# First transform half: 24 narrow low parts moved from VectorE to GpSimd, with fixed PSUM banks and a new order

## The chip, the cores and the metric

The kernel runs on one core of a Trainium2 chip. The metric is device time in microseconds (us) of one launch; the kernel before was timed in three runs, and their median is the number that the change is compared with. A core has five engines that each work through a queue of their own, in order: TensorE (PE), VectorE (DVE), ScalarE (ACT), GpSimd (POOL) and SyncE (SP, which issues DMAs). They wait for each other only where data or a buffer demands it.

## The reference

```python
xn = layernorm(x)                                  # x: 2048 x 576
a  = xn @ dft_hid_re.T;   b = xn @ dft_hid_im.T    # 2048 x 576 each
y  = dft_seq_re @ a - dft_seq_im @ b               # the two 2048 x 2048 products
m  = relu(xn @ w1) @ w2                            # 576 -> 4608 -> 576
out = x + y + m
```

## The kernel before

Every float32 matrix is split into two float16 parts, a high part (the value cast to float16) and a low part (value minus high part), and a product is three float16 matmuls: high by high, high by low, low by high. Products are laid out as a seven-product block scheme (Strassen-Winograd): seven half-size products, with sums of blocks made beforehand or added afterwards.

The program runs through nine blocks of the MLP (`b` 0 to 8, four token groups `g` each; `t = 4b + g` up to 35), then through the transform. The transform has two halves. In the first half, for each token tile `t` from 0 to 15 and each half `z` of the columns, seven products (`pd`, L1392) of the normalised input and the hidden DFT matrix accumulate in three PSUM banks; they are collected (scaled by a half) into a float32 buffer `tb`, which has room for four tiles: tiles 4 to 7 use the places of 0 to 3. In the second half, sixteen units multiply blocks of the sequence DFT matrix (`cs`, its split parts) by these results (`R`, their split parts), L1478. Units 0 to 7 need tiles 0 to 7 only, so the first half is done in two goes: tiles 0 to 7 ahead of unit 0, tiles 8 to 15 around unit 7 and 8.

How one tile `t` of the first half becomes the right operand `R[t]`:

- `q:t:z:n` is product `n` (7 matmuls). A pair of tiles `t` and `t+2` is made by the products of `t`, so only `t` = 0, 1, 4, 5 stand in the table, 56 products in all.
- `c:t:z:n` collects it. Products 2, 3 and 7 are added by DVE from PSUM (L1405); the others are copied by ACT (L1407) or, marked V, by DVE (L1409).
- `sh:t:s` is a high part, on ACT (L1361). For `s` = 11, 21, 22 it is narrow, 128x288; for `s` = 0 it is wide, 128x1152: the four sums of blocks.
- `sl:t:s` is the low part, on DVE (L1365), with two inputs: the value in `tb` and the high part.
- `rs:t` makes the four sums in place in `tb` (DVE, L1371 to L1374), and so must come after the three narrow low parts of its tile have read it, and after the collection of product 4. The wide parts follow it.
- Unit steps: `oh` (ACT, L1015) and `ol` (DVE, L1019) split a left operand, `os` (DVE, L1447) makes its sums, `u:n:i:h` is one half (12 matmuls) of product `i` of unit `n`, `ue` evicts it, `ua` adds it to DRAM by a DMA issued on POOL.

The last MLP blocks and the first half, up to the end of unit 6, are written out word by word in a table, BLOCK8, which sets the order of all five queues; the rest is in another table, TURN. In BLOCK8 the words `p`, `f`, `h`, `l`, `x`, `H`, `L` are first-layer products and their activations, `m` a second-layer product (L809), `e` its eviction, `a:t:n` the DMA on POOL that adds it to DRAM, and `dl`, `dx`, `dL`, `dh`, `dw`, `ds` load, measure and split the hidden DFT matrix.

PSUM has eight banks. In the transform, `bank()` hands out tiles of two pools of four (`ps1`, `psd`) in turn, in the order in which the program asks.

Of the kernel before, what the change touches and what calls it, by code (L numbers as in the profile page):

```python
# [148 lines left out]
e:31:1 p:32:1:3 h:32:1:12 a:31:1 dl:2 l:32:1:12 m:31:3 f:32:1:3 dx:1:1 r:32:1 x:32:1 p:32:0:4
dx:1:0 p:33:0:5 h:32:0:12 m:31:2 l:32:0:12 f:33:0:5:A y:32:0 y:32:1 H:32:0 p:33:0:1 e:31:2:V  # L150
S:32:1 p:33:1:1 f:33:0:1:V L:32:0 e:31:3:A m:31:4 F:33:0 H:32:1 f:33:1:1:V m:31:5 e:31:4 L:32:1
a:31:4 dl:3 m:31:6 e:31:5 dx:2:1 a:31:5 m:32:0 e:31:6:V S:33:0 dx:2:0 a:31:6 p:33:1:6 F:33:1
m:32:1 f:33:1:6:V p:33:0:3 p:33:0:2 p:33:0:6 f:33:0:2 e:32:0:A p:33:1:2 f:33:0:6:V dL:0:0
h:33:0:11 f:33:0:3 m:32:2 f:33:1:2 r:33:0 e:32:1 h:33:1:11 l:33:1:11 a:32:1 p:33:0:7 l:33:0:11
dx:3:1 p:33:1:7 f:33:0:7 m:32:3 x:33:0 h:33:0:22 e:32:2:A l:33:0:22 dx:3:0 p:33:0:4 p:33:1:5
y:33:0 h:33:0:12 dR:0 l:33:0:12 H:33:0 m:32:4 f:33:1:5:V dp:0 S:33:1 f:33:1:7 L:33:0 p:34:0:1
e:32:3:A dL:0:1 p:33:1:4 f:34:0:1:A e:32:4 dh:0:0:1 p:33:1:3 h:33:1:12 dw:0:0:1 a:32:4 h:33:1:22
m:32:5 l:33:1:12 dh:0:0:0 f:33:1:3 F:34:0 r:33:1 dw:0:0:0 p:34:0:5 e:32:5 m:32:6 l:33:1:22
a:32:5 ds:0:0 dh:0:1:1 m:33:0 dh:0:1:0 dw:0:1:1 dh:0:0:2 x:33:1 p:34:0:6 e:32:6:A p:34:0:2
dh:0:0:3 f:34:0:5:V a:32:6 dw:0:0:2 m:33:1 dw:0:0:3 S:34:0 f:34:0:2 dL:0:2 p:34:0:3 f:34:0:6:V  # L160
dw:0:1:0 e:33:0:A p:34:0:7 y:33:1 h:34:0:11 e:33:1 H:33:1 p:34:1:2 f:34:0:7 a:33:1 p:34:1:1
l:34:0:11 h:34:0:22 L:33:1 p:34:0:4 F:34:1 f:34:1:1:A p:34:1:6 f:34:1:2 h:34:0:12 f:34:0:3
h:34:1:11 ds:0:1 m:33:2 r:34:0 m:33:3 e:33:2:A f:34:1:6:V dL:1:2 x:34:0 dh:0:1:3 m:33:4 dh:0:2:1
l:34:0:12 e:33:3:A y:34:0 dw:0:1:3 dh:0:1:2 m:33:5 e:33:4 H:34:0 l:34:0:22 a:33:4 dh:0:2:0
L:34:0 p:34:1:7 S:34:1 p:34:1:5 dw:0:2:0 p:35:0:1 F:35:0 f:34:1:5:V l:34:1:11 p:34:1:3
f:35:0:1:V dw:0:2:1 m:33:6 f:34:1:3 e:33:5 r:34:1 f:34:1:7 a:33:5 p:35:0:5 e:33:6:A x:34:1
p:34:1:4 h:34:1:22 a:33:6 l:34:1:22 p:35:0:2 y:34:1 h:34:1:12 f:35:0:5:A l:34:1:12 p:35:0:6
H:34:1 f:35:0:2 ds:0:2 p:35:1:1 h:35:0:11 S:35:0 p:35:1:2 m:34:0 F:35:1 l:35:0:11 dh:0:2:2
f:35:0:6:V dw:0:1:2 dh:0:2:3 p:35:0:7 dw:0:2:2 dL:1:0 e:34:0:V p:35:0:3 f:35:0:7 m:34:1 dw:0:2:3
h:35:0:22 f:35:0:3 L:34:1 r:35:0 p:35:0:4 p:35:1:5 e:34:1 h:35:0:12 S:35:1 m:34:2 x:35:0 a:34:1  # L170
y:35:0 dL:1:1 m:34:3 l:35:0:22 e:34:2:A f:35:1:1:V f:35:1:2 H:35:0 l:35:0:12 pm:0 m:34:4
e:34:3:A L:35:0 h:35:1:11 f:35:1:5:A p:35:1:6 e:34:4 p:35:1:3 l:35:1:11 f:35:1:6:A a:34:4
p:35:1:7 f:35:1:3 r:35:1 m:34:5 f:35:1:7 x:35:1 h:35:1:22 p:35:1:4 e:34:5 m:34:6 l:35:1:22
dh:1:2:0 a:34:5 y:35:1 h:35:1:12 dw:1:2:0 dh:1:1:1 m:35:0 dh:1:0:1 e:34:6:V dh:1:1:0 l:35:1:12
a:34:6 dh:1:0:0 m:35:1 dh:1:2:1 dw:1:1:1 dw:1:1:0 H:35:1 dw:1:2:1 dw:1:0:1 q:0:0:1 e:35:0:A
L:35:1 q:0:0:2 e:35:1 m:35:2 ds:1:1 a:35:1 q:0:0:5 e:35:2:A m:35:3 dw:1:0:0 dh:1:1:3 dh:1:1:2
ds:1:0 m:35:4 e:35:3:A dw:1:1:2 m:35:5 dh:1:0:2 e:35:4 dh:1:0:3 dw:1:0:2 m:35:6 a:35:4 e:35:5
dw:1:0:3 a:35:5 e:35:6:A dw:1:1:3 a:35:6 fs:0 q:0:1:1 ds:1:2 fm:0 c:0:0:5:A cl:0:0 q:1:0:1
c:0:1:1:A q:0:0:3 c:1:0:1:A c:0:0:1:V dh:1:2:2 q:1:0:6 c:0:0:2 dh:1:2:3 dw:1:2:2 q:0:0:6 sh:0:11
dw:1:2:3 c:1:0:6:A q:0:1:6 c:0:0:6:A sl:0:11 c:0:0:3 pa:0 q:0:0:7 c:0:1:6:A pb:0 sh:2:11 q:0:1:5  # L180
sl:2:11 c:0:0:7 pc:0 q:0:1:7 c:0:1:5:V pd:0 q:0:1:3 c:0:1:7 q:1:1:1 sh:2:22 c:0:1:3 sl:2:22
sh:2:21 q:1:1:2 c:1:1:1:A sl:2:21 rs:2 q:0:1:4 q:0:1:2 c:0:1:4:A sh:0:22 q:1:1:5 sh:2:0 sl:0:22
c:1:1:2 q:0:0:4 c:0:1:2 sh:1:21 sl:2:0 sh:0:21 q:1:1:6 c:1:1:5:A c:0:0:4:A q:1:1:3 sl:1:21
c:1:1:6:A sl:0:21 q:1:0:5 c:1:1:3 rs:0 sh:3:21 q:1:1:7 c:1:0:5:A q:1:0:3 sl:3:21 q:1:0:2 sh:0:0
c:1:1:7 c:1:0:3 q:1:1:4 c:1:0:2 sh:3:22 sl:0:0 sh:3:11 q:1:0:7 sh:1:11 c:1:1:4:A q:4:0:1 sh:1:22
c:1:0:7 sl:3:11 q:1:0:4 sl:1:22 c:4:0:1:A sl:3:22 q:4:0:2 rs:3 c:1:0:4:A fx:0 cl:0:2 oh:0 cl:0:3
q:4:0:5 cl:0:1 q:4:1:1 c:4:0:5:A ol:0 sh:3:0 q:4:1:5 sl:1:11 c:4:1:1:A q:4:1:2 sl:3:0 c:4:1:5:A
q:4:1:3 c:4:1:2 q:4:0:3 rs:1 sh:4:21 oh:1 q:4:1:6 q:5:0:1 sl:4:21 sh:1:0 ol:1 q:5:0:2 c:4:1:6:A
q:4:0:6 c:4:1:3 sl:1:0 sh:6:21 q:4:1:7 c:4:0:6:A q:4:0:7 c:5:0:1:A c:4:1:7 os:0:0 sh:6:22
q:5:0:6 q:4:1:4 c:4:0:7 c:5:0:6:A sl:6:22 os:0:1 q:4:0:4 c:4:1:4:A sh:4:22 q:5:0:7 c:4:0:2  # L190
# [24 lines left out]
ue:5:1 u:5:2:1 ol:40 ua:5:1 u:5:3:0 ue:5:2:V oh:41 cl:7:2 ol:41 u:5:3:1 u:5:4:0 oh:42 ue:5:3:A
ol:42 u:5:4:1 cl:7:1 os:6:1 u:5:5:0 oh:43 ue:5:4 ol:43 ua:5:4 u:5:5:1 os:6:2 u:5:6:0 oh:44
# [62 lines left out]
def kernel(  # L279
# [1188 lines left out]
    def block_product(n, i, ks):  # L1468
# [3 lines left out]
        if first and ks.start == 0:  # L1472
            places[n, i] = bank(f"p{n}_{i}")
# [131 lines left out]
```

## Time and profile before

| What | before |
|---|---|
| time, median of 3 runs | 1228.23 us (1227.09 to 1229.61) |
| span of the profiled execution (first to last instruction) | 1226.3 us |
| busy: PE, DVE, ACT, POOL | 1215.1, 1055.6, 726.2, 210.5 us |
| granted TensorE clock | 1.000 |

The profile gives the span of the execution that it shows; the time of a run includes what lies around the span, so the three runs lie 0.8 to 3.3 us above the span, the median 1.9 us. PE is busy in 99% of the span: the kernel can only lose or win in stretches where PE waits.

### The profile page before, as it was taken

Reading aid. Unit: us, or ns where it says so; the run is one execution under the profiler, and the core shown is the slowest. Engines: PE = TensorE matmul, PEld = TensorE weight load, DVE = VectorE, ACT = ScalarE, POOL = GpSimd, SP = SyncE. Lnnn points to the kernel's source line nnn. Section 1 sums busy time; section 2 is a strip of 40 time slices with the busy share of each in tenths; the row PEclk is TensorE's granted clock in tenths of the full one; section 3 lists DMA queues with packets and bytes.
Section 4 is the critical chain, followed back from the end, with each engine's and each line's share of the span. In section 5 each row is a group of like instructions: output and inputs, shape, how many; then the busy total and the mean of one; then the engine's idle time right before and its main releaser. Section 6 shows DMA issues by size and latency. Waiting matters only on the chain.

```text
span 1226.3 us, 26245 instructions
## 1 busy us (share of the span) xinstructions
PE 1215.1 (99%) x10516; PEld 999.2 (81%) x10516; DVE 1055.6 (86%) x2044; ACT 726.2 (59%) x1259; POOL 210.5 (17%) x274
## 2 busy tenths in 40 slices
PE   8999999999999999999999999998999999999998
PEld 8867888888888888888888888876777777777777
DVE  8877998888888889888988889999877769987885
ACT  7866765766757667657666547666444445534342
POOL 3432122122122222221121111200211110000000
PEclk9999999999999999999999999999999999999999
DMA  8997578688778777777666678631755532245441
GB/s 239 223 165 194 161 142 177 147 162 146 159 145 176 151 138 167 138 146 151 150 120 140 153 177 164 116 90 49 192 131 135 132 79 47 91 157 181 142 132 35
DMA packets 127051, 175.98 MB, mean 144 GB/s; under 512 B 48336, under 2 KB 88784, under 8 KB 126928
## 3 DMA queue, kind: packets, MB, share of 16 engines
q1 hardware_dynamic: 97696, 121.99, 34.0%
q0 software_dynamic: 28672, 51.92, 30.0%
q8 instruction: 82, 1.34, 0.5%
q10 hardware_dynamic: 560, 0.39, 0.1%
q14 instruction: 41, 0.34, 0.1%
HBM read 112.53 MB, written 56.62 MB: 138 GB/s over the span
## 4 chain that ended last, share of the span: by engine, by line
PE 94%; DVE 3%; DMA 1%; ACT 0%; issue 0%; SPq 0%; POOL 0%; DVEq 0%; ACTq 0%
PE bank L712 27%; PE p L809 27%; PE p L1478 26%; PE pd L1392 7%; PE p L588 4%; PE p L849 2%; DMA raw_w<-in_w_dram 1%; DVE R L1365 1%; PE p L1074 1%; DMA xT<-dbuf 0%; DVE w2s L1019 0%; DVE cs L1019 0%; DVE tb L1405 0%; DVE accs L1447 0%; DVE tb L1372 0%
## 5 line engine op out<-in xcount | busy, mean ns | idle before, releaser
L809 PE MATMUL p<-w2s,h 128*128 128x288 f16 x2688 | 357.0, 286 | 0.0
L1478 PE MATMUL p<-R,cs 128*128 128x288 f16 x2688 | 331.0, 286 | 2.5 <-DVE cs L1019 2.5
L1478 PEld LDWEIGHTS <-cs 128*128 128x128 f16 x2688 | 262.8, 98 | 69.6 <-DVE cs L1019 3.4
L809 PEld LDWEIGHTS <-h 128*128 128x128 f16 x2688 | 263.0, 98 | 62.0
L712 PEld LDWEIGHTS <-dbuf 128*128 128x128 f16 x1568 | 153.2, 98 | 20.7 <-issue 0.4
L712 PEld LDWEIGHTS <-wbuf 128*128 128x128 f16 x1568 | 153.4, 98 | 20.4
L1015 ACT ACTIVATE cs<-tb,sc_c 128x1024 f16<-128x1024 f32 x56 | 64.3, 1148 | 82.1 <-PE p L1478 59.8
L712 PE MATMUL bank<-xT,wbuf 128*128 128x256 f16 x896 | 110.4, 273 | 0.0
L712 PE MATMUL bank<-xT,dbuf 128*128 128x256 f16 x896 | 110.2, 273 | 0.0
L1019 DVE SCALAR_TENSOR_TENSOR cs<-tb,sc_c,cs 128x1024 f16<-128x1024 f32 x56 | 71.7, 1283 | 22.2 <-ACT cs L1015 21.3
L834 POOL DMA_DIRECT2D spill<-dbuf x70 | 61.3, 915 | 163.0 <-DVE dbuf L827 119.9
L712 PE MATMUL bank<-accs,dbuf 128*128 128x256 f16 x672 | 86.3, 273 | 0.2 <-DVE s L738 0.2
L712 PE MATMUL bank<-accs,wbuf 128*128 128x256 f16 x672 | 85.9, 273 | 0.0
L1015 ACT ACTIVATE cs<-accs,sc_c 128x1024 f16<-128x1024 f32 x40 | 45.9, 1148 | 58.5 <-PE p L1478 45.7
L759 DVE TENSOR_TENSOR h<-s,h 128x1024 f16<-128x1024 f32 x64 | 77.4, 1218 | 2.1 <-ACT h L753 2.1
L753 ACT ACTIVATE h<-s 128x1024 f16<-128x1024 f32 x64 | 66.6, 1050 | 13.1 <-DVE s L750 13.1
L1239 ACT ACTIVATE f<-f 128x1024 f32<-128x1024 f32 x64 | 67.2, 1050 | 4.0 <-DMA f<-in_cim_dram 3.0
L721 ACT ACTIVATE h<-accs 128x256 f16<-128x256 f32 x128 | 51.1, 410 | 29.9 <-DVE accs L736 23.7
L834 POOL DMA_DIRECT2D spill<-wbuf x42 | 39.5, 940 | 155.9 <-DVE wbuf L827 128.2
L1019 DVE SCALAR_TENSOR_TENSOR cs<-accs,sc_c,cs 128x1024 f16<-128x1024 f32 x40 | 51.2, 1282 | 13.7 <-ACT cs L1015 13.5
L823 ACT ACTIVATE dbuf<-p,c_ub 128x576 f32<-128x576 f32 x61 | 45.0, 738 | 25.5 <-PE p L809 25.5
L702 ACT ACTIVATE accs<-bank 128x256 f32<-128x256 f32 x97 | 36.9, 380 | 38.2 <-PE bank L712 15.6
(227 smaller groups left out, 1897.8 us busy)
## 6 DMA issues: line engine op xcount, KB each, us to landing
spill<-dbuf POOLq DMA_DIRECT2D x80, 288.0 KB, 4.5
f<-in_cre_dram SPq DMA_DIRECT2D x32, 512.0 KB, 5.0
f<-in_cim_dram SPq DMA_DIRECT2D x32, 512.0 KB, 5.0
spill<-wbuf POOLq DMA_DIRECT2D x48, 288.0 KB, 5.5
raw_w<-in_w_dram SPq DMA_DIRECT2D x18, 576.0 KB, 4.8
raw_w<-in_w_dram SPq DMA_DIRECT2D x17, 512.0 KB, 4.7
accs<-in_cim_dram SPq DMA_DIRECT2D x16, 512.0 KB, 4.6
tb<-in_cre_dram SPq DMA_DIRECT2D x16, 512.0 KB, 4.6
```

The costliest lines, as they stand in the source:

```text
L588: nc.tensor.matmul(ps[:, cols], w1s[b, i // 2][:, i % 2 * 2 + h, y], xT[g][:, h * KC + z, cols], start=(n == 0), stop=(n == len(wk) - 1),)
L712: nc.tensor.matmul(ps, l, r, start=first and m == 0, stop=m == len(todo) - 1, skip_group_check=not first,)
L721: nc.scalar.activation(next(high_low(q)), SOURCE[q], AF.Relu)
L753: order["s"] = nc.scalar.activation(next(high_low(SUMS)), stage_of(slice(1, 5)), AF.Copy).ins
L759: order["lo"] = nc.vector.tensor_tensor(lo, stage_of(slice(1, 5)), hi, ALU.subtract).ins
L809: nc.tensor.matmul(ps[:, c], h[:, x, qa, c * P : (c + 1) * P], w[:, y, qb], start=first and i == 0 and j == 0, stop=i == NQ - 1 and j == 2 ...
L834: nc.gpsimd.dma_start(spill[g, row, col], sums[g, row, col], accum_op=ALU.add)
L1015: nc.scalar.activation(hi, src, AF.Copy, scale=s)
L1019: nc.vector.scalar_tensor_tensor(lo, src, s, hi, ALU.mult, ALU.subtract)
L1239: nc.scalar.activation(f, f, AF.Abs, scale=2.0**-10, accum_out=sums_c[:, n, q : q + 1])
L1392: nc.tensor.matmul(ps, x[:, k, c * P : (c + 1) * P], dsp[z][:, a, y], start=first and m == 0, stop=m == len(PASSES) - 1, skip_group_check= ...
L1478: nc.tensor.matmul(ps, w[:, a, RANK[k]], r[:, c, RIGHT[rq]], start=first and k == 0 and j == 0, stop=k == HK - 1 and j == 2, skip_group_ch ...
```

## The change

- The 24 narrow low parts of tiles 0 to 7 get the word `:G` and run on GpSimd. They were 24 of 32 low parts on DVE there; the eight wide ones stay on DVE. Those of tiles 8 to 15 (in TURN) stay on DVE too.
- `bank()` is gone. All eight banks are allocated under numbers, and two tables say which three banks each chain of the first half and each unit uses.
- BLOCK8 is replaced up to unit 2 by the same words in a new order: 929 words in both, the only other difference being the `:G`. Among the moves: the first tile pair starts with product 2; the adds `a:35:4` to `a:35:6` go later, between the low parts on POOL; `a:31:4` goes from right behind its eviction to late in the last block; the loads `cl` of the left operands and the half units `u` are interleaved anew. From unit 3 on, and in TURN, the order is unchanged.

```diff
 BLOCK8 = """
...
-dw:1:2:3 c:1:0:6:A q:0:1:6 c:0:0:6:A sl:0:11 c:0:0:3 pa:0 q:0:0:7 c:0:1:6:A pb:0 sh:2:11 q:0:1:5
...
+sh:2:22 c:0:0:6:A q:0:0:7 q:0:1:4 c:0:1:4:A c:0:0:2 sh:0:11 sl:0:11:G c:0:0:3 q:1:1:1 sh:2:11
...
 """
+BANKS_D = "312 067 451 210 765 403 125 467 312 074 672 103 564 732 017 644"
+BANKS_C = "032 167 453 201 675 430 127 564 312 054 761 230 546 713 024 657"
...
-    def low_part(t, s):
+    def low_part(t, s, eng=nc.vector):
         hi, lo, src = part(t, s)
-        tt(lo, src, hi, ALU.subtract)
+        eng.tensor_tensor(lo, src, hi, ALU.subtract)
...
         if (t, z) not in chains:
-            chains[t, z] = [bank(f"pd{t}_{z}_{k}") for k in range(3)]
+            k = 2 * (t // TG * 2 + t % 2) + z
+            chains[t, z] = [bank_at[int(k)] for k in BANKS_D.split()[k]]
...
-            places[n, i] = bank(f"p{n}_{i}")
+            places[n, i] = bank_at[int(BANKS_C.split()[n][(0, 1, None, 2)[i]])]
...
-        pool["psd"] = tc.alloc_tile_pool(name="psd", bufs=4, space=PSUM)
+        pool["psd"] = tc.alloc_tile_pool(name="psd", bufs=1, space=PSUM)
+        for k in range(4, 8):
+            bank_at[k] = pool["psd"].tile([P, 512], F32, name=f"bank{k}")
```

Two places show what the table does to the queues. The first is DVE's queue where the first sums of a tile are made. In before these are the sums of tile 2 (`tb` has no numbers of its tiles), with a narrow low part (L1365, 128x288) after nearly every addition from PSUM (L1405):

```order
L1405 SCALAR_TENSOR_TENSOR tb_10831<-pd0_1_2_10814,tb_10831 128x288
L1365 TENSOR_TENSOR R2_10834<-tb_10831,R2_10834 128x288 x2
L1371 TENSOR_TENSOR tb_10831<-tb_10831 128x288
L1372 TENSOR_TENSOR tb_10831<-tb_10831 128x288
L1373 TENSOR_TENSOR tb_10831<-tb_10831 128x288
L1374 TENSOR_TENSOR tb_10831<-tb_10831 128x288
L1365 TENSOR_TENSOR R0_10832<-tb_10831,R0_10832 128x288
L1405 SCALAR_TENSOR_TENSOR tb_10831<-pd1_1_1_10936,tb_10831 128x288
L1405 SCALAR_TENSOR_TENSOR tb_10831<-pd0_1_1_10813,tb_10831 128x288
L1365 TENSOR_TENSOR R2_10834<-tb_10831,R2_10834 128x1152
```

The same place now, where the first sums are those of tile 0 (additions are L1404 here, sums L1369 to L1372):

```order
L1404 SCALAR_TENSOR_TENSOR tb_10806<-bank7_10821,tb_10806 128x288
L1404 SCALAR_TENSOR_TENSOR tb_10806<-bank0_1783,tb_10806 128x288
L1404 SCALAR_TENSOR_TENSOR tb_10806<-bank6_10820,tb_10806 128x288
L1369 TENSOR_TENSOR tb_10806<-tb_10806 128x288
L1370 TENSOR_TENSOR tb_10806<-tb_10806 128x288
L1371 TENSOR_TENSOR tb_10806<-tb_10806 128x288
L1372 TENSOR_TENSOR tb_10806<-tb_10806 128x288
L1404 SCALAR_TENSOR_TENSOR tb_10806<-bank3_1786,tb_10806 128x288
```

The narrow low parts are gone from DVE, and the first sums come after more additions: the one from `bank0` collects product 2 of tile 1, the one from `bank6` product 2 of tile 0 in its second column half.

The second place is POOL's queue at the end of the last MLP block. In before it holds DMAs alone, the last adds of the MLP (L834) and then those of the units (L1502):

```order
L834 DMA spill_00_113<-sums 128x576
L834 DMA spill_11_116<-sums 128x576
L834 DMA spill_01_114<-sums 128x576
L834 DMA spill_10_115<-sums 128x576
L1502 DMA spill_00_101<-accs 128x288
```

Now a configuration step (ISA) and the low parts (L1363) stand there, and three of the adds among them:

```order
L838 DMA spill_00_113<-sums 128x576
L1363 ISA
L1363 TENSOR_TENSOR R_10807<-tb,R_10807 128x288 x2
L838 DMA spill_11_116<-sums 128x576
L838 DMA spill_01_114<-sums 128x576
L1363 TENSOR_TENSOR R_10809<-tb,R_10809 128x288 x2
L1363 TENSOR_TENSOR R_10807<-tb,R_10807 128x288
L1363 TENSOR_TENSOR R_10809<-tb,R_10809 128x288
L1363 TENSOR_TENSOR R_10810<-tb,R_10810 128x288
L838 DMA spill_10_115<-sums 128x576
L1363 TENSOR_TENSOR R_10810<-tb,R_10810 128x288 x2
```

More of the change, by code (lines that the diff above doesn't have):

```diff
@@ L149 @@
[L149 to L178, printed above, removed]
@@ L666, in transpose_sums @@
                 nc.sync.dma_start_transpose(dst, st[:, q].rearrange("p k c -> p (k c)"))
-    banks1 = []
+    banks1, bank_at = [], {}
     def freed(i, key="free"):
@@ L679, in pair_products @@
                 banks1.append((bank[:, :GH], bank[:, GH:]))
+                bank_at[(1, 0, 3, 2)[k]] = bank
         u, v, w = (banks1[k][0] for k in (i, 2, 3))
@@ L1339, in right_of @@
         return RT[k]
-    banks = [0]
-    def bank(name):
-        src, tag = ((ps1, "ps1"), (pool.get("psd"), "psd"))[banks[0] // 4 % 2]
-        banks[0] += 1
-        return src.tile([P, 512], F32, tag=tag, name=name)
     def block_of(t):
```

126 lines of the change are left out of this document (78 added, 48 removed).

## The prediction

> **What bounds the kernel now.** I read the page first, then a table by stretches around the changed words, then PE's, DVE's and POOL's timelines there.
>
> ```profile
> PE 1215.1 (99%) x10516; PEld 999.2 (81%) x10516; DVE 1055.6 (86%) x2044; ACT 726.2 (59%) x1259; POOL 210.5 (17%) x274
> ```
>
> PE is busy in all but 11.2 us of the span, and the change takes no matmul away. So the question is where PE waits. By stretches (busy us of PE, PEld, DVE, ACT, POOL, then clock and DMA):
>
> ```profile
> 690.00:796.00 106.00, 106.00 (x908) 88.58 (x907) 96.54 (x197) 59.33 (x109) 19.09 (x23) 1.00 0.74 152
> 796.00:811.70 15.70, 15.69 (x126) 12.14 (x126) 14.29 (x35) 9.05 (x21) 0.85 (x1) 1.00 0.44 86
> 811.70:857.60 45.90, 42.51 (x341) 32.82 (x339) 44.84 (x80) 29.75 (x51) 0.00 (x0) 1.00 0.20 63
> 857.60:905.00 47.40, 47.40 (x388) 37.86 (x389) 40.33 (x41) 21.05 (x22) 8.54 (x10) 1.00 0.71 180
> ```
>
> Up to 811.7 and after 857.6 PE has no gap; between them it has 3.4 us of gaps while DVE works 98% of the time. PE's timeline there (start, us, what; in brackets the gap ahead and what ended it), and two rows of the chain of waits for PE's own pace:
>
> ```profile
> 839.15 1.02 PE L1392 MATMUL pd<-dbuf,accs 128*128 128x288 f16 x7
> ...
> 843.09 1.02 PE L1392 MATMUL pd<-dbuf,accs 128*128 128x288 f16 x7 [0.80 <-DVE tb L1405]
> 843.95 4.82 PE L1478 MATMUL p<-R,cs 128*128 128x288 f16 x38
> 849.82 3.18 PE L1478 MATMUL p<-R,cs 128*128 128x288 f16 x24 [1.05 <-DVE cs L1019]
> 853.55 3.12 PE L1478 MATMUL p<-R,cs 128*128 128x288 f16 x24 [0.55 <-DVE cs L1019]
> 857.57 52.60 PE L1478 MATMUL p<-R,cs 128*128 128x288 f16 x428 [0.90 <-DVE cs L1019]
> ```
>
> ```profile
> 802.58 25.85 PE pd L1392 x210
> 857.57 52.48 PE p L1478 x427
> ```
>
> A product of seven matmuls takes 25.85/30 = 0.862 us, a matmul of the units 52.48/427 = 0.123. From 839.15 to 857.57, 18.42 us, PE does four products and 86 unit matmuls, 14.0 us: 4.4 us are lost, all to DVE, and the last wait that ends is for the low part of a left operand (`ol:4`, L1019) ahead of half unit `u:0:4:0` at 857.57. Without the loss that would start at 853.2. This 4.4 us (0.36%) is all that the changed words can gain.
>
> **The change, part by part.** DVE's queue is what counts. It has no wait but 0.3 us from the first row here to the last:
>
> ```profile
> 811.75 0.45 DVE L1371 TENSOR_TENSOR tb<-tb 128x288 f32<-128x288 f32 x1
> 812.23 0.46 DVE L1372 TENSOR_TENSOR tb<-tb 128x288 f32<-128x288 f32 x1
> ...
> 828.45 0.46 DVE L1405 SCALAR_TENSOR_TENSOR tb<-pd,tb 128x288 f32<-128x288 f32 x1 [0.26 <-PE pd L1392]
> ...
> 856.23 1.28 DVE L1019 SCALAR_TENSOR_TENSOR cs<-accs,sc_c,cs 128x1024 f16<-128x1024 f32 x1
> ```
>
> The first is the start of `rs:0`, the last is `ol:4`: 45.8 us from there to PE's restart. What DVE's words cost, from the chain (it runs along DVE here, so the rows are paces):
>
> ```profile
> 843.40 1.47 DVE R L1365 x4
> 844.87 0.38 DVE tb L1371
> ...
> 846.72 0.38 DVE tb L1371
> ...
> 849.76 2.54 DVE R L1365 x2
> ```
>
> A narrow low part takes 1.47/4 = 0.37 us, four sums (844.87 to 846.72) 1.85, a wide low part 1.27.
>
> *Removed from DVE.* 24 x 0.37 = 8.9 us. But it isn't all in the stretch that decides. From `rs:0` to `ol:4`, before has 17 narrow low parts, 7 `rs` and 7 wide ones; after has 0, 8 and 8 (tile 2 now follows tile 0), and as many additions, `ol`, `os` and evictions. So 45.8 - 6.3 + 1.85 + 1.27 = 42.6 us.
>
> *When that stretch starts.* In the new order `rs:0` stands behind the collection of product 2 of tile 1, second half, which is 17 products behind PE's first product of tile 0's second half. PE's row for that one in before, whose place is nearly the same in both orders:
>
> ```profile
> 794.96 1.02 PE L1392 MATMUL pd<-wbuf,xT 128*128 128x288 f16 x7
> ```
>
> It ends at 795.98; 17 x 0.862 and 0.3 for two small matmuls later it is 810.9, and two additions at 0.37 follow: `rs:0` starts at 811.7, as before. So what DVE saves ahead of it becomes waiting for PE. Then 811.7 + 42.6 = 854.3 against 857.57: a gain of 3.3 us, if DVE isn't slowed.
>
> *Added on POOL.* Its nearest rows are the low parts of the first stage (512 and 64 wide), and the DMA issues:
>
> ```profile
> L521 POOL TENSOR_TENSOR wbuf<-x,wbuf 128x512 f16<-128x512 f32 x3 | 3.4, 1150 | 0.0
> L520 POOL TENSOR_TENSOR wbuf<-x,wbuf 128x64 f16<-128x64 f32 x3 | 0.9, 298 | 17.0 <-ACT wbuf L515 17.0
> L834 POOL DMA_DIRECT2D spill<-sums x16 | 13.6, 853 | 55.7 <-DVE sums L827 50.5 <-ACT sums L823 2.8 <-DVE wbuf L1209 2.0
> L1134 POOL PARTITION_ALL_REDUCE z<-eps x1 | 2.1, 2127 | 6.7 <-issue 6.7
> ```
>
> Between 64 and 512 columns it is 1.9 ns a column, so 288 take 0.73 us: 24 x 0.73 and three DMA issues at 0.85 are 20 us of work in a stretch of some 40: POOL itself is no limit. The configuration step is priced by the last row: 6.7 us without work and a first instruction of 2.1. It stands behind `a:35:1`, which POOL issued here:
>
> ```profile
> 787.80 0.85 POOL L834 DMA_DIRECT2D spill<-sums  x1 [2.89 <-DVE sums L827]
> ```
>
> So POOL is ready at about 797.5, and the first low part isn't needed before `rs:0` at 811.7: nothing. If it came late, `rs:0` would wait, up to 2 us. The adds `a:35:4` to `a:35:6` land later, but what reuses their buffer (the operand of tile 7) is 20 us behind them: nothing.
>
> *DVE and POOL together.* This is the term that decides, and before has no such stretch. It has single meetings in the first stage. Both engines' timelines, and the groups that give the normal durations:
>
> ```profile
> 82.47 1.26 DVE L925 SCALAR_TENSOR_TENSOR dbuf<-raw_w,c_sw,dbuf 128x512 f16<-128x512 f32 x1 [0.58 <-ACT dbuf L920]
> 82.02 1.16 POOL L521 TENSOR_TENSOR wbuf<-accs,wbuf 128x512 f16<-128x512 f32 x1
> L925 DVE SCALAR_TENSOR_TENSOR wbuf<-raw_w,c_sw,wbuf 128x512 f16<-128x512 f32 x28 | 20.7, 738 | 0.4 <-ACT wbuf L920 0.4
> 27.11 2.14 POOL L655 TENSOR_TENSOR accs<-accs,first_xn 128x512 f32<-128x512 f32 x2 [7.06 <-DVE accs L655]
> 27.16 0.67 DVE L521 TENSOR_TENSOR dbuf<-accs,dbuf 128x512 f16<-128x512 f32 x1
> L655 POOL TENSOR_TENSOR accs<-accs,first_xn 128x512 f32<-128x512 f32 x1 | 1.9, 1864 | 7.1 <-DVE accs L655 7.1
> L655 POOL TENSOR_TENSOR accs<-accs 128x512 f32<-128x512 f32 x5 | 6.4, 1273 | 0.1
> 45.30 0.68 DVE L611 SCALAR_TENSOR_TENSOR h<-p,h 128x512 f16<-128x512 f32 x1
> 45.04 1.16 POOL L521 TENSOR_TENSOR dbuf<-accs,dbuf 128x512 f16<-128x512 f32 x1
> ```
>
> DVE's L925 has two inputs in SBUF; started while POOL worked, it took 0.52 us longer than its 0.738 and so began its work at 82.99, when POOL was nearly done. POOL's L655, started beside such a DVE instruction, took 1.86 in place of 1.27. But L611, whose input is in PSUM, took its usual 0.68 in the middle of a POOL instruction. So an instruction of DVE with two SBUF inputs and one of POOL exclude each other: POOL holds what they share for its duration less some 0.15, 0.58 us here. DVE's sums, wide low parts, `ol` and `os` are all of that kind; only the additions and evictions from PSUM aren't.
>
> From `rs:0` on 20 of the 24 low parts on POOL are to come. By DVE's order, 12 fall where the next row of DVE is of the excluded kind: each costs DVE 0.58 less the 0.12 that a sum waits for the one before it anyway (the sums start 0.48 apart, 811.75 to 812.23, the low parts 0.37), 0.46. Eight fall ahead of an addition, which hides 0.37 of them: 0.2. Together 5.5 + 1.6 = 7.1 us. The bounds are 0, if DVE always has an addition to do (it has 16 in the stretch, 5.9 us), and 20 x 0.73 = 14.6. I take 7.1, since the rows show full exclusion in both directions.
>
> The Trainium skill, "SBUF — State Buffer", section "SBUF: two separate sides", says that a DVE instruction with two SBUF inputs and a GpSimd instruction lock each other out of a shared port pair, for the whole instruction. The rows agree but for the last word: L925 got in 0.19 us before POOL's row ends. What the whole duration would make of the sum is the third rival.
>
> *The rest.* The fixed banks remove and add no instruction; PE waits for none before 839, so they can gain nothing there, and where a bank is reused at once (`q:1:0:5` after an addition that DVE does on time) up to 0.5 us could be lost: 0. The last MLP block moves its words, but PE has no gap from 690 to 796 in before and DVE 9.5 us of idle: 0, with up to 1 us to lose.
>
> The sum: -3.3 + 7.1 = +3.8 us, PE's restart at 861.4. The profiled span of 1226.3 becomes 1230.1; the median of the runs lies 1.9 above the span, so 1228.2 + 3.8 = 1232.0.
>
> **Rivals.**
>
> - DVE isn't slowed: POOL's instructions fall into DVE's additions and waits. Against it: DVE has no waits after `rs:0`. Then only the 3.3 us gain is left: 1224.9. The sign turns where a POOL instruction costs DVE 3.3/20 = 0.17 us.
> - Half cover: each POOL instruction costs 0.2, as the eight do: 4.0 - 3.3, 1228.9, no change.
> - The whole duration is lost, 0.73 and not 0.58: 12 x 0.61 + 8 x 0.36 = 10.2, and 10.2 - 3.3 = +6.9, 1235.1. L925 speaks against it. POOL's own lateness, with `rs` waiting for its low parts, would cost alike.
>
> **How the numbers follow.** Forecast 0.40, no slowing 0.20, half cover 0.25, whole duration 0.15. A change under 0.2% (2.5 us) can't be told from none. Slower by more: most of the forecast (0.32) and the whole duration (0.15), 0.48 with a little of half cover. Same: 0.22 of half cover and 0.08 of the forecast, 0.30. Faster: 0.20 and a little more, 0.22. The range runs from the case without slowing, 1224.5, to 1237.0, past the third rival but short of 14.6 - 3.3 = +11.3; the forecast's own is 1229.5 to 1235.
>
> **What the profile after would show.** DVE's sums (0.46 us) and wide low parts (1.35) lengthened beside POOL's instructions, and these longer than 0.73; `rs:0` at 811.7 and DVE without waits after it; PE's gaps before `u:0:4:0` at 8 us in place of 4.4. If sums keep their 0.46 beside POOL, the first rival holds. A PE gap before 796, or waits of DVE for POOL of more than 1 us, would make the prediction wrong in another way.

## The result, and the profile after

| | before | changed kernel |
|---|---|---|
| time, median of six runs each | 1228.25 us (1227.09 to 1230.90) | 1239.66 us (1237.02 to 1243.33) |
| ratio | | 1.0089 (95%: 1.0072 to 1.0105) |
| span of the profiled execution | 1226.3 us | 1240.6 us |

The change costs 11.4 us. The forecast of 1232.0 had the sign right and the size not; 1239.66 lies above its range. The profiled execution of the changed kernel is one of its slower ones: 1242.57 us, 2.9 over the median.

The changed kernel's page, first row, and its table by the stretches that the prediction shows of before (columns as there):

```profile
PE 1219.8 (98%) x10516; PEld 1001.4 (81%) x10516; DVE 1057.6 (85%) x2020; ACT 723.3 (58%) x1259; POOL 233.7 (19%) x298
690.00:796.00 106.00, 103.73 (x887) 86.42 (x885) 92.63 (x192) 57.46 (x108) 18.48 (x22) 1.00 0.70 151
796.00:811.70 15.70, 15.55 (x126) 12.09 (x124) 12.22 (x24) 6.56 (x13) 0.00 (x0) 1.00 0.31 84
811.70:857.60 45.90, 39.33 (x312) 30.04 (x311) 39.93 (x61) 27.66 (x57) 25.97 (x27) 1.00 0.26 54
857.60:905.00 47.40, 45.26 (x355) 35.13 (x353) 38.77 (x43) 19.73 (x20) 4.09 (x5) 0.96 0.47 135
```

Three things are new. PE now has gaps in the last MLP block (2.3 us from 690 to 796, none before). In the transform's stretch PE's gaps are 8.7 us from 811.7 to 905, 3.4 before. And behind that the granted clock falls below 1 for some microseconds. PE's timeline, the main rows with a gap ahead of them:

```profile
705.36 0.93 PE L716 MATMUL bank<-accs,wbuf 128*128 128x256 f16 x7 [0.27 <-DVE accs L708]
767.74 1.69 PE L716 MATMUL bank<-xT,wbuf 128*128 128x256 f16 x14 [1.04 <-DVE accs L738]
769.91 1.69 PE L716 MATMUL bank<-xT,wbuf 128*128 128x256 f16 x14 [0.49 <-DVE h L729]
...
826.65 1.02 PE L1391 MATMUL bank<-dbuf,accs 128*128 128x288 f16 x7 [2.21 <-DVE tb L1404]
...
839.48 1.02 PE L1391 MATMUL bank<-wbuf,accs 128*128 128x288 f16 x7 [1.78 <-DVE tb L1404]
...
861.26 0.40 PE L1477 MATMUL bank<-R,cs 128*128 128x288 f16 x2 [1.08 <-ACT accs L1491]
862.72 69.22 PE L1477 MATMUL bank<-R,cs 128*128 128x288 f16 x550 [1.06 <-DVE cs L1023]
933.32 66.92 PE L1477 MATMUL bank<-R,cs 128*128 128x288 f16 x545 [1.38 <-ACT accs L1491]
```

DVE's and POOL's timelines show the meetings: a sum of DVE (L1372) that takes 2.92 us instead of 0.46 beside three low parts of POOL in a row, six low parts that take 7.43 us instead of 6 x 0.73, and DVE waiting for the last POOL low part of a tile before its sums:

```profile
817.27 0.61 DVE L1369 TENSOR_TENSOR tb<-tb 128x288 f32<-128x288 f32 x1
...
823.32 2.92 DVE L1372 TENSOR_TENSOR tb<-tb 128x288 f32<-128x288 f32 x1
...
856.69 0.97 DVE L1369 TENSOR_TENSOR tb<-tb 128x288 f32<-128x288 f32 x1 [1.32 <-POOL R L1363]
812.53 0.73 POOL L1363 TENSOR_TENSOR R<-tb,R 128x288 f16<-128x288 f32 x1 [17.72 <-PE bank L1391]
...
823.52 2.38 POOL L1363 TENSOR_TENSOR R<-tb,R 128x288 f16<-128x288 f32 x3
...
850.82 7.43 POOL L1363 TENSOR_TENSOR R<-tb,R 128x288 f16<-128x288 f32 x6 [5.07 <-ACT R L1359]
```

The first sums (`rs:0`) start at 817.27, 5.6 us behind the forecast's 811.7.

**A difference to take out first.** The words of the first 130 us are the same in all these kernels, and yet the profiled executions come out of that stretch up to several us earlier or later. From 130 to 690 us PE has next to no gap in any profile here (0.1 us at most; 4853 to 4858 matmuls in 560 us, 0.1153 us each), so the matmuls done by 130 us tell how late an execution starts into the rest. Rows of the table by stretches for before, the changed kernel, and two experiments below (banks_alone, mended):

```profile
0.00:130.00 130.00, 125.46 (x1310) 98.99 (x1311) 106.47 (x288) 92.73 (x169) 45.84 (x74) 1.00 0.90 206
0.00:130.00 130.00, 125.02 (x1295) 98.88 (x1296) 108.87 (x285) 90.81 (x164) 44.12 (x74) 1.00 0.89 206
0.00:130.00 130.00, 124.58 (x1285) 98.65 (x1286) 103.49 (x283) 89.98 (x161) 46.33 (x74) 0.99 0.90 204
0.00:130.00 130.00, 121.13 (x1252) 94.69 (x1253) 105.15 (x274) 87.67 (x157) 43.32 (x72) 0.99 0.88 197
```

The changed kernel's profiled execution is 15 matmuls late there, 1.7 us; of its 14.3 us over before, 12.6 come later. Of these PE's gaps make 2.4 (690 to 800), 5.3 (811.7 to 905, 8.7 against 3.4) and 1.4 (933.32), and the lower clock about 1.6 (550 unit matmuls in 69.22 us, at 0.123 they take 67.7). Some 2 us are not placed.

### The profile page after: what moved, and what is told of

Its sections match the earlier page's. It is cut to its first block, busy times and chain, and to the rows that moved or that the text cites. A ratio compares the mean times of both kernels' runs of the same rounds, so it can differ in the third digit from the quotient of the medians.

```text
span 1240.6 us, 26262 instructions
## 1 busy us (share of the span) xinstructions
PE 1219.8 (98%) x10516; PEld 1001.4 (81%) x10516; DVE 1057.6 (85%) x2020; ACT 723.3 (58%) x1259; POOL 233.7 (19%) x298
## 4 chain that ended last, share of the span: by engine, by line
PE 86%; DVE 5%; DMA 4%; ACT 2%; issue 2%; POOL 1%; SPq 0%; ACTq 0%; DVEq 0%
PE bank L716 26%; PE bank L1477 25%; PE p L813 24%; PE bank L1391 5%; PE p L853 3%; PE p L591 3%; DMA raw_w<-in_w_dram 1%; DMA xT<-dbuf 1%; DMA spill<-accs 1%; DVE tb L1370 0%; POOL R L1363 0%; DMA raw_dk<-in_dft_dram 0%; DVE cs L1023 0%; DVE tb L1404 0%; DVE tb L1371 0%
## 5 line engine op out<-in xcount | busy, mean ns | idle before, releaser
L1477 PE MATMUL bank<-R,cs 128*128 128x288 f16 x2688 | 332.5, 287 | 3.5 <-ACT accs L1491 2.5
L1023 DVE SCALAR_TENSOR_TENSOR cs<-accs,sc_c,cs 128x1024 f16<-128x1024 f32 x40 | 51.3, 1284 | 13.8 <-ACT cs L1019 13.7
```

The source lines that it names most:

```text
L1023: nc.vector.scalar_tensor_tensor(lo, src, s, hi, ALU.mult, ALU.subtract)
L1477: nc.tensor.matmul(ps, w[:, a, RANK[k]], r[:, c, RIGHT[rq]], start=first and k == 0 and j == 0, stop=k == HK - 1 and j == 2, skip_group_ch ...
```

## The experiments

Each kernel was timed against before on one chip. "Later" is its profiled span less before's 1226.3, without the start's share by the count of matmuls (0.1153 us each): one execution, so it stands beside the median.

| run | median | over before, timed with it | ratio, 95% | later |
|---|---|---|---|---|
| changed kernel | 1239.66 | 11.4 | 1.0072 to 1.0105 | 12.6 |
| pool_alone | 1238.53 | 9.9 | 1.0061 to 1.0087 | 8.4 |
| order_alone | 1242.11 | 13.5 | 1.0096 to 1.0125 | 14.8 |
| banks_alone | 1230.71 | 2.1 | 1.0003 to 1.0020 | 0.0 |
| no_pool | 1244.32 | 15.7 | 1.0101 to 1.0135 | 11.9 |
| pool_early | 1233.16 | 3.7 | 1.0019 to 1.0040 | 3.2 |
| pool_memset | 1231.35 | 1.9 | 1.0006 to 1.0023 | 0.5 |
| pool_scalar | 1234.69 | 5.4 | 1.0028 to 1.0056 | 5.0 |
| old_mlp | 1234.56 | 5.1 | 1.0031 to 1.0061 | 5.4 |
| new_mlp | 1233.33 | 3.9 | 1.0020 to 1.0043 | 3.9 |
| old_mlp_no_pool | 1239.20 | 9.9 | 1.0069 to 1.0096 | 8.8 |
| old_mlp_memset | 1227.32 | -2.0 | 0.9974 to 0.9992 | -2.2 |
| old_mlp_old_banks | 1235.73 | 6.5 | 1.0042 to 1.0068 | 6.4 |
| s35_late | 1242.83 | 11.8 | 1.0080 to 1.0113 | 13.5 |
| s_late | 1243.93 | 12.9 | 1.0092 to 1.0130 | 15.9 |
| adds_early | 1242.75 | 13.0 | 1.0093 to 1.0129 | 13.8 |
| adds_s | 1238.66 | 8.9 | 1.0063 to 1.0088 | 11.7 |
| a35_early | 1239.75 | 10.5 | 1.0069 to 1.0094 | 11.1 |
| mended | 1241.25 | 12.0 | 1.0061 to 1.0097 | 9.9 |

### The three parts alone

**pool_alone**: before, with the low parts on POOL.

```diff
-... sl:2:22 ... sl:0:11 ...
+... sl:2:22:G ... sl:0:11:G ...
```

> Before with the 24 narrow low parts on GpSimd, old order, old banks. In the profile of the changed kernel DVE's rows between the first sums and the last left operand ahead of the units are lengthened by 8.1 us beside GpSimd. If that meeting is the cause (theory 1), 6.3 us leave DVE's queue here and some 8 come back: 1230 or, with waits for GpSimd added, up to 1237. If the new order is the cause (theory 2), GpSimd's part is about even: 1226 to 1230. If the fixed banks are (theory 3): 1224 to 1228.

It costs 9.9 us. Its profile shows a cost that the changed kernel hides, POOL's configuration step. POOL's timeline, then PE's:

```profile
799.55 0.85 POOL L838 DMA_DIRECT2D spill<-sums  x1 [0.21 <-issue]
811.14 3.90 POOL L1369 TENSOR_TENSOR R<-tb,R 128x288 f16<-128x288 f32 x5 [10.75 <-ACT tb L1411]
816.34 1.84 PE L1396 MATMUL pd<-wbuf,accs 128*128 128x288 f16 x7 [5.16 <-DVE tb L1409]
817.98 1.83 PE L1396 MATMUL pd<-dbuf,accs 128*128 128x288 f16 x7
```

In the old order the step stands behind the last MLP add (799.55) and POOL does nothing for 10.75 us; DVE's sums wait for its first low parts, PE for DVE (5.16 us), and two products then take 1.84 and 1.83 us instead of 1.02. The bracket names the event of ACT that came last. The first low part's own input, a high part, was ready at 803.3 (ACT's row at 802.87, 0.43 us long), so of the 10.75 us POOL would have waited 2.9 without the step, too.

**pool_early** puts one small tensor_tensor on POOL behind the MLP's last all-reduce, so that the step runs early:

```diff
         yield from power(sc["d"], pw["d"], m)
+        z = small.tile([P, 1], F32, tag="z", name="z")
+        nc.gpsimd.tensor_tensor(z, eps, eps, ALU.subtract)
```

> Pool_alone with one GpSimd tensor_tensor of 128x1 more, right behind the last all-reduce of the MLP, so that GpSimd's configuration step runs some 60 us earlier. In pool_alone the step began at 800.2 and the first low part only at 811.1; DVE waited 4.3 us for it, PE 5.2 us, and PE ran 3.5 us at half clock behind that. Theory 1 (two GpSimd costs: the step and the meetings with DVE): the 5.2 us and some 1.7 us of half clock go: 1231 to 1233. Rival (the meetings alone, the wait comes back further on): 1236 to 1239.

Here the step leaves POOL without work for 7.32 us, in an earlier place. POOL's row, and one of PE's behind it:

```profile
745.20 0.37 POOL L1174 TENSOR_TENSOR z<-eps 128x1 f32<-128x1 f32 x1 [7.32 <-issue]
759.59 1.63 PE L813 MATMUL p<-w2s,h 128*128 128x288 f16 x12 [1.05 <-ACT sums L827]
```

The 5.16 us gap is gone and the time is 6.2 us nearer to before. The earlier place isn't free: two adds that pool_alone issues at 741.46 and 744.13 go out together at 745.53, ACT waits 1.09 us for such an add and 1.33 us for a load, and PE has the gap of 1.05 us at 759.59, while pool_alone, whose PE rows are the same up to there, has none. So some 1 us of the 3.7 that remain is likely still the step's, and the rest is what the move of the low parts costs in the old order. In the changed kernel the step starts at 795 and the first low part at 812.53, right behind ACT's high part that it needs (812.01, 0.44 us long): hidden, as predicted.

**order_alone**: before with the changed kernel's word table, all low parts on DVE. **no_pool**: the changed kernel with `:G` taken off all 24 words, so the fixed banks too. **banks_alone**: the changed kernel with before's table, so the fixed banks alone.

```diff
 # order_alone                     # no_pool                  # banks_alone
-BLOCK8 = (before)                -sl:0:11:G                 +BANKS_D, BANKS_C, bank_at
+BLOCK8 = (changed, without :G)   +sl:0:11                    BLOCK8 = (before)
```

> Before with the new order alone: low parts on DVE, banks handed out in turn. Theory 1 (DVE and GpSimd meet): 1228, as before, and no PE gaps ahead of 796 us. Theory 2 (the order): the 2.3 us of PE gaps in the last MLP block stay, rs:0 starts 3 us or more late and the low parts are still on DVE behind it: 1232 to 1238. Theory 3 (banks): 1228 to 1230.

> The changed kernel with its 24 low parts back on DVE (new order and fixed banks stay). Theory 1: 7.4 us of low parts come back behind the first sums, 8.1 us of lengthening and 1.3 us of waiting go, and with them the stretch of half clock behind the last gap (2 us): 1234 to 1236, and no sum of DVE longer than 0.5 us. Theory 2: the order sets the end, 1237 to 1241. Theory 3: as theory 2.

> Before with the fixed banks alone. Theories 1 and 2: 1227 to 1229, the banks cost nothing in the old order. Theory 3: the PE waits for an eviction by ACT that the changed kernel shows (1.1 us at 861 and 1.4 us at 933) come from the banks, and more of them in an order they were not chosen for: 1230 to 1236.

The order alone costs 13.5 us, and no_pool 15.7: both more than any of the cases expected. On the new order low parts on POOL seem a gain (15.7 us without them, 11.4 with them, but the intervals touch; with the old MLP words, below, 9.9 and 5.1 are clear of each other), while on the old order they are a loss. DVE then waits for ACT's high parts, 5.3 us in no_pool (groups of instructions, 808 to 868 us):

```profile
L1363 DVE TENSOR_TENSOR R<-tb,R 128x288 f16<-128x288 f32 x24 | 10.3, 454 | 5.6 <-ACT R L1359 5.3
```

The banks' 2.1 us are more than the 1227 to 1229 expected without a cost, but they are not in the changed words: PE's gaps behind 800 are before's to the hundredth, and all of the later span is in the first 130 us (25 matmuls late, row above), where the words are the same. Both profiled executions lie within 0.4 us of their kernel's median, so the later start may go with the kernel and not only with the execution; why is open. With the old banks in the changed transform (old_mlp_old_banks, below) the time isn't lower either.

### The low parts on POOL without their meetings

**pool_memset** and **pool_scalar**: the changed kernel, with each POOL low part replaced (the product lacks its low terms, or has wrong ones).

```diff
-        eng.tensor_tensor(lo, src, hi, ALU.subtract)
+        eng.memset(lo, 0.0)                                  # pool_memset
+        eng.tensor_scalar(lo, src, 1.0, None, ALU.mult)      # pool_scalar
```

> The changed kernel with each of the 24 low parts on GpSimd replaced by a memset of the same 128x288 tile: no input, no configuration step, and nothing for the sums to wait for (the low parts are zero, so the product lacks their terms). It shows what the move would give without meetings and waits. Theory 1: 8.1 us of lengthened DVE rows, 1.3 us of waiting and the 2 us of half clock go, the 2 to 3 us lost in the last MLP block and the later waits stay: 1228 to 1231. Rival (the new order sets the end whoever makes the low parts): 1237 or more.

> The changed kernel with each low part on GpSimd replaced by a tensor_scalar of one input (the value times one, 128x288, float32 to float16; the product's low terms are wrong by that). If only GpSimd instructions of two inputs shut DVE out: DVE's sums keep 0.46 us and the time is 1231 to 1234, like the memsets plus the sums' wait for GpSimd. If any read of SBUF by GpSimd does: sums of 0.6 us in the mean and 1238 to 1241, as in the changed kernel.

The memsets take away 9.5 of the 11.4 us. They remove the meetings, and with them the waits of POOL for high parts and of DVE for POOL. The groups for one of the four sums, from 808 to 868, in the changed kernel, pool_memset and pool_scalar (count, total, mean):

```profile
L1372 DVE TENSOR_TENSOR tb<-tb 128x288 f32<-128x288 f32 x8 | 6.1, 765 | 0.4
L1375 DVE TENSOR_TENSOR tb<-tb 128x288 f32<-128x288 f32 x8 | 3.7, 458 | 0.3
L1375 DVE TENSOR_TENSOR tb<-tb 128x288 f32<-128x288 f32 x8 | 4.1, 509 | 0.4
```

Beside memsets the sums keep 0.458 us. Beside one-input instructions of POOL they take 0.51 (0.48 to 0.54 for all four), although POOL works longer than in the changed kernel:

```profile
L1363 POOL TENSOR_TENSOR R<-tb,R 128x288 f16<-128x288 f32 x24 | 24.8, 1104 | 36.8 <-ACT R L1359 19.1 <-PE bank L1391 17.7
L1364 POOL TENSOR_SCALAR R<-tb 128x288 f16<-128x288 f32 x24 | 29.1, 1245 | 27.0 <-ACT R L1359 14.5 <-DVE tb L1407 10.5 <-ACT tb L1409 1.9
```

So what lengthens DVE's sums is mostly the second input of POOL's instruction; the expectation of 0.46 us held nearly, the time came 0.7 over it. The two engines still meet: a one-input instruction takes 0.93 us while DVE is idle (at 813.78) and 1.25 in the mean, so here it is POOL that is held up. DVE and POOL thus wait for each other where neither data nor a buffer demands it. The Trainium skill, "SBUF — State Buffer", section "SBUF: two separate sides", has a GpSimd instruction that reads SBUF and a DVE instruction with two SBUF inputs block each other for a whole instruction. The memsets and the two-input rows agree with it; the sums beside one-input instructions, nearly as short as alone, do not.

### The two halves of the order

The words up to the first collection of the transform (398 in before, 392 in the changed kernel) are called the MLP words. **old_mlp** is the changed kernel with the MLP words in before's order, **new_mlp** is before with them in the new order. The adds `a:35:4` to `a:35:6` are MLP words in before, so old_mlp also takes them out from between the low parts; in new_mlp they stand in a row behind the MLP words.

```diff
 # old_mlp                            # new_mlp
-BLOCK8 = new MLP words + new rest   -BLOCK8 = old MLP words + old rest
+BLOCK8 = old MLP words + new rest   +BLOCK8 = new MLP words + old rest
```

> The changed kernel (GpSimd and fixed banks too) with the words of the last MLP blocks, up to the first collection of the transform, in the order of before, and the new order from there. Theory: the new order of the MLP words costs 2.3 us of PE gaps and some 0.5 of order: 1236 to 1237.5. Rival: what it arrives earlier with is waited away in the transform: 1239 to 1240.

> Before with the words of the last MLP blocks, up to the first collection of the transform, in the new order; the transform, the low parts on DVE and the banks as before. If the 4.0 us of PE gaps that the order alone shows from 690 to 800 us belong to these words: 1231 to 1233, and if DVE falls behind for the transform's words too, up to 1236. Rival (the loss lies in the transform's order): 1228 to 1229.

Both show it: 6.3 us less in the one (more than was expected, and give or take some 3 by the intervals), 3.9 more in the other. Old_mlp's table by stretches has no PE gap ahead of 811.7:

```profile
690.00:796.00 106.00, 106.00 (x908) 88.56 (x907) 96.51 (x196) 59.78 (x110) 19.91 (x24) 1.00 0.74 151
796.00:811.70 15.70, 15.70 (x128) 12.18 (x127) 8.69 (x23) 7.22 (x18) 2.94 (x6) 1.00 0.47 108
811.70:857.60 45.90, 38.77 (x305) 29.52 (x304) 42.90 (x62) 26.81 (x50) 22.75 (x20) 1.00 0.10 36
```

**old_mlp_memset** and **old_mlp_no_pool** are old_mlp with the memset of pool_memset, and with `:G` taken off; **old_mlp_old_banks** is old_mlp with `bank()` handing out tiles in turn.

```diff
 # old_mlp_memset           # old_mlp_no_pool   # old_mlp_old_banks
-eng.tensor_tensor(...)    -sl:0:11:G          -[bank_at[int(k)] for k in BANKS_D.split()[k]]
+eng.memset(lo, 0.0)       +sl:0:11            +[bank(f"pd{t}_{z}_{k}") for k in range(3)]
```

> Old_mlp with the memsets of pool_memset in place of GpSimd's low parts (their terms are missing from the product): the new order of the transform with neither meetings nor MLP gaps. By the sum of the parts (1231.4 less the 4 to 5 us that the MLP words cost): 1226 to 1228, PE gaps of under 2 us behind 800. Rival (parts don't add, the order has a cost of its own): 1230 or more.

> Old_mlp with the 24 low parts back on DVE: the old MLP words, the new order of the transform's words, the fixed banks. If the new transform order is itself slower and GpSimd's low parts win part of it back (no_pool against the changed kernel: 4.7 us): 1238 to 1241, with DVE waiting for high parts of ACT (5.3 us in no_pool). Rival (the loss of the order was all in the MLP words): 1230 to 1232.

> Old_mlp with the banks handed out in turn again. The fixed banks cost 2.1 us in the old order and 2.2 in the new without GpSimd, with PE gaps that do not differ. If that holds here: 1232 to 1233. Rival (they cost nothing, the 2 us were scatter of the first 130 us): 1234 to 1235.

Old_mlp_memset is the one kernel below before: -2.0 us. It shows what the new transform order is worth when the low parts cost nothing, and old_mlp, 7.1 us above it (give or take some 2), what they cost on POOL. The half unit `u:0:4:0`, PE's last restart in the prediction, stands behind 98 unit matmuls in before and in both of these. DVE's first row of `rs:0` and PE's row of `u:0:4:0`, in old_mlp and then in old_mlp_memset:

```profile
811.03 0.45 DVE L1369 TENSOR_TENSOR tb<-tb 128x288 f32<-128x288 f32 x1
861.27 61.67 PE L1477 MATMUL bank<-R,cs 128*128 128x288 f16 x502 [0.31 <-DVE cs L1023]
813.64 0.45 DVE L1372 TENSOR_TENSOR tb<-tb 128x288 f32<-128x288 f32 x1
856.10 61.67 PE L1480 MATMUL bank<-R,cs 128*128 128x288 f16 x502 [0.26 <-DVE cs L1023]
```

Old_mlp's execution starts 0.9 us ahead of before's and old_mlp_memset's 1.6 behind it; with that taken out the restarts are at 862.2 and 854.5, against 857.57 in before. Between its two rows old_mlp's DVE is lengthened by 6.0 us (the 32 sums by 4.3, the wide low parts by 1.2, two other rows by 0.5) and waits 1.31 us for POOL; its 17 additions from PSUM keep their 0.45 us.

Old_mlp_no_pool shows that this order is made for POOL: with DVE doing the low parts it is 9.9 us slower than before. Since the parts that gain compute less than the reference, no complete version faster than before came out of the experiments.

### What in the MLP words costs it

Two of them stand out in the table: the loads that ACT measures (words S) come 2 to 24 words behind their load (F) instead of 14 to 46, and the adds (words a) mostly 10 to 93 words behind their eviction, a:31:4 251, instead of 1 to 5. S_late's ACT and PE rows show what a late add does:

```profile
716.24 0.74 ACT L826 ACTIVATE dbuf<-p,c_ub 128x576 f32<-128x576 f32 x1 [4.35 <-DMA spill<-dbuf]
717.03 3.04 PE L812 MATMUL p<-w2s,h 128*128 128x288 f16 x12 [3.02 <-ACT dbuf L826]
```

ACT's eviction into `dbuf` waits for the add that still reads it, and PE waits for ACT. In the changed kernel's own profile the same eviction (ACT at 713.07) waits 1.40 us for PE and not for the add, so this wait is what the late adds can do, not what is shown to cost the changed kernel its time. POOL issued these adds at 698.11 and 700.65 in before, together at 706.86 in the changed kernel:

```profile
698.11 0.85 POOL L834 DMA_DIRECT2D spill<-dbuf  x1 [8.34 <-DVE dbuf L827]
700.65 0.86 POOL L834 DMA_DIRECT2D spill<-dbuf  x1 [1.70 <-DVE dbuf L827]
706.86 2.07 POOL L838 DMA_DIRECT2D spill<-dbuf  x2
```

Six kernels move such words of the changed kernel: **s35_late** (one S), **s_late** (all S), **adds_early** (the adds of the MLP words to one word behind their evictions), **adds_s** (both), **a35_early** (the three adds between the low parts), **mended** (adds_s and a35_early).

```diff
-F:35:0 ... dh:0:2:3 S:35:0 dw:0:1:3 ...          # s35_late
+F:35:0 ... dh:1:0:0 L:35:0 S:35:0 ...
-e:30:4 ... (35 words) a:30:4                      # adds_early
+e:30:4 p:31:1:4 a:30:4
-sl:0:22:G ... a:35:4 ... a:35:5 ... a:35:6        # a35_early
+e:35:6:A ... a:35:4 a:35:5 a:35:6 ... sl:0:11:G
```

> The changed kernel with one word moved: S:35:0 (ACT's measuring of a sequence DFT block, which waits for its load) 22 words later. In the changed kernel ACT waited 2.4 us for that load at 761.4, its activation of DVE's next input came late, DVE waited 1.6 us and PE 1.0 and 0.5 us at 767.7 and 769.9. If the load brought early into ACT's queue is what those gaps come from: they vanish (1.5 us) and the time is 1236 to 1238.5 against 1239.7. Rival (DVE's own words are late): the gaps stay, 1239 to 1241.

> The changed kernel with all eight words S of the last MLP blocks some 14 words later (their loads have more time before ACT waits for them). If these words carry the loss of the MLP order: PE's gaps from 690 to 800 fall from 2.4 us to under 1, 1234 to 1237. Rival (other words do): 1238 to 1241.

> The changed kernel with the adds of the last MLP blocks (words a, DMAs issued by GpSimd) moved back to one word behind their evictions; in the new order they stand up to 36 words behind (a:31:4 251). In s35_late and s_late ACT waited 2.8 and 4.4 us at about 715 for the DMA that such an add makes from dbuf, and PE 1.5 and 3.0 us for ACT. If the late adds carry the loss: the waits of ACT for these DMAs go, PE's gaps from 690 to 800 fall to 1.5 us (what stands at 767 to 772), 1235 to 1238. Rival (other words): 1239 to 1242.

> Adds_early with the words S 14 later too, as in s_late. If the adds and the loads waited for are all that is wrong with the MLP words: PE's gaps from 690 to 800 under 1 us and the time of old_mlp, 5.1 us over before: 1233.5 to 1236. Rival (the rest of the order costs as much): 1238 or more.

> The changed kernel with three adds alone moved: a:35:4 to a:35:6, which the change put between the low parts in GpSimd's queue, back to where they were, ahead of the configuration step. In the changed kernel they hold up the low parts, three of which then run back to back at 823.5 and stretch one sum of DVE to 2.92 us, behind which PE waits 2.2 us; old_mlp, which has them early, shows neither. If the adds do that: the 2.92 us sum and the 2.2 us gap go, 1236.5 to 1238.5 against 1239.7 (some 8 to 9.5 us over before). Rival (the step, now later, makes the first low part late, or the wait comes back): 1239 to 1242, 10 us or more over before.

> Adds_s with a:35:4 to a:35:6 back ahead of the configuration step too. Adds_s was 8.9 us over before with the same 2.2 us gap. If late adds, early loads and these three adds make up what old_mlp takes away: 5 to 7 us over before, 1234 to 1236.5. Rival: 8 us or more over before.

All six came out above what was expected if their words were the cause. None of s35_late, s_late and adds_early is faster than the changed kernel. S35_late keeps the gaps it was to remove, s_late makes them small and shows 3 us for the late add instead, adds_early removes the wait for the add and shows PE gaps of 1.48 and 1.27 us at 766 to 769, ahead of which DVE waited 3.5 us for ACT, and ACT 2.4 us for a load. Adds_s is lower, 8.9 us over before, and a35_early takes the 2.92 us sum and the 2.21 us PE gap away in its profile, as expected, but little of the time (10.5 us over before); the ratios of both overlap the changed kernel's.

Mended's six runs lie from 1235.15 to 1244.76, and its profiled execution starts 58 matmuls, 6.7 us, late; without the start it is at 9.9, against 12.6 for the changed kernel and 5.4 for old_mlp. These 2.7 us aren't won in the MLP block: PE's gaps from 690 to 800 are 2.3 us there, as against 2.4. From 811.7 to 905 they are 7.5 instead of 8.7, and most of the rest is the clock, which in this execution isn't lowered. Of the 7.2 us between the changed kernel and old_mlp, 2.4 are gaps ahead of 800, 1.3 gaps from 811.7 to 905, 0.8 the wait for ACT's eviction behind them (1.38 against 0.55 us), and 1.6 the lower clock. Which of the MLP words make up their cost is open.

## Why the prediction was wrong

*The sum of the transform's part held.* It had -3.3 us for the move without slowing; old_mlp_memset shows -2.0, and its PE restarts at 854.5 where 854.3 was forecast. It had +7.1 for DVE and POOL shutting each other out; old_mlp against old_mlp_memset shows 7.1, and old_mlp restarts at 862.2 where 861.4 was forecast. Together +3.8 was forecast and +5.1 is old_mlp's time over before. That 7.1 agrees to the tenth is luck: the rows give 6.0 of lengthening, and 1.3 of waiting for POOL that the sum did not have. "DVE isn't slowed", the rival on the other side, is excluded by the rows of the sums.

*The step that failed is "The rest"*: "The last MLP block moves its words, but PE has no gap from 690 to 796 in before and DVE 9.5 us of idle: 0, with up to 1 us to lose". It measured 6.3 us (changed kernel against old_mlp) and 3.9 (new_mlp against before). With the 1.3 us that the transform's part came out higher, the 6.3 make up the 7.6 us between 3.8 and 11.4. PE's gaps from 690 to 800 went from none to 2.4 us in both kernels with the new MLP words. The forecast took the slack of the old order for a property of the stretch. It looked at PE's gaps and DVE's idle sum, and not at the other two queues that the moved words stand in: ACT, which waits in order for loads and adds, and POOL, on which most adds moved 10 words or more later. Which of these words carries the cost the runs don't show. A part of the 6.3 us may belong to the three adds `a:35:4` to `a:35:6`, which the prediction had put at nothing: without them between the low parts PE's gaps from 811.7 to 905 are 7.2 us in a35_early instead of 8.7, though its median shows no clear gain. The prediction's own last sentence named both signs that came, a PE gap before 796 and a wait of DVE for POOL of more than 1 us.

*`rs:0`* was to start at 811.7. Old_mlp has it at 811.03, its profiled execution 8 matmuls, 0.9 us, ahead; so the chain of 17 products behind PE was right, and the changed kernel's 817.27 is PE's lateness from the start and the MLP words.

*POOL's configuration step* at nothing: right here. Its price was put at 6.7 us without work by the row of another stage; it is 7.32 in pool_early and up to 10.75 in pool_alone, where it did come late, in the old order, and DVE's sums waited 4.27 us for the low parts and PE 5.16 for DVE.

*Fixed banks* at 0: right by the profiles.

*What the profile after would show*: sums and POOL instructions lengthened (yes: means 0.59 to 0.77 and 1.10 us), PE's gaps at 8 us in place of 4.4 (in gaps alone 8.7 from 811.7 to 905 in place of 3.4, and 7.4 in old_mlp), DVE without waits behind `rs:0` (no: 1.32 us for POOL, 0.41 for PE). Not foreseen were the half clock behind the gaps (about 1.6 us here), and the waits for ACT's unit evictions (1.08 and 1.38 us), which stand in ACT's queue behind wide high parts that wait for DVE's sums.

## What to carry to other kernels

Price a reordering by queue: for each word that moves, ask what stands behind it on every engine and which buffer its DMA holds, and don't take a stretch without gaps as one with slack, since its order may be what keeps it so. Two-input work moved from DVE to POOL relieves DVE only where DVE's instructions beside it have at most one SBUF input; sized from a few single meetings in another stage, that cost came out at 7.1 us for 20 instructions where the rows show 6.0, and 7.3 with a wait. A profile's start can differ between kernels that begin with the same words: count the matmuls done at a fixed time and compare what is behind it.

## What the hardware showed unexpectedly

The granted clock fell to half after short gaps, and not always. The changed kernel's clock column, 862 to 868 us, behind gaps of 1.08 and 1.06 us with two matmuls between them:

```profile
862.00:864.00 2.00, 1.28 (x8) 0.90 (x9) 2.00 (x3) 0.66 (x1) 0.00 (x0) 0.80 0.04 8
864.00:866.00 2.00, 2.00 (x10) 1.29 (x9) 2.00 (x2) 0.00 (x0) 0.00 (x0) 0.50 0.00 0
866.00:868.00 2.00, 2.00 (x16) 1.46 (x15) 2.00 (x4) 1.58 (x2) 0.00 (x0) 0.85 0.87 236
```

The middle row has ten matmuls in 2 us. S_late, adds_early, adds_s, a35_early and old_mlp_old_banks have these gaps and the lower clock, too: 550 matmuls in 69.2 us behind them. Old_mlp, s35_late and mended have the same two gaps (in old_mlp at 853.38 and 854.84) and keep the full clock: 48 matmuls in 6.12 us and 502 in 61.67. The gap of 2.21 us at 826.65 keeps it in the changed kernel, while in s35_late the same gap (2.22 us) is followed by a clock of 0.50. So up to 1.6 us of the difference between two of these profiles can be the clock alone. The Trainium skill, "TensorE: Matmul & The Clock Gate", section "Part 1: The HAM clock gate", puts the fall behind an idle window of about 3.4 us; here 2.1 us of idle in 2.5 were enough in six profiles and not in three.

A run of POOL instructions once held a DVE sum for all of its length: three low parts, 2.38 us, and a sum of 2.92. Beside the six low parts in a row from 850.82 the sums got in between, at 0.97 and 0.87 us. And the change of configuration left POOL without work for 6.7, 7.32 and 10.75 us in three places (2.9 of the last POOL would have waited for its input); by what its length varies is open.
